# Scratch rows of four runs side by side, and an input read by four transfers for each half batch

## The chip, the cores and the metric

The kernel runs on one core of a Trainium2 chip. The metric is the device time of one execution in microseconds (us). Runs of the same kernel agree within some tenths of a per cent.

## What is computed

Two layers, one behind the other, in float32. The first is a causal convolution over time with a softmaxed kernel of 7 taps for each of 8 heads. The second is a layer of 8 experts in which the (token, expert) pairs are taken in the order of their gate values and an expert takes at most 3584 tokens.

```python
def _attn_ref(x, weight):             # x 8 x 3584 x 192, weight 8 heads x 7 taps
    w = softmax(weight)               # over the taps
    x_pad = np.concatenate([np.zeros((B, 6, D)), x], axis=1)
    ...
    out = np.einsum('hk,bskhg->bshg', w, x_unf)

def _moe_ref(x, w_gate, w1, w2):      # x 28672 x 192, 8 experts, inner width 1024
    order = np.argsort(-(x @ w_gate).flatten())
    for idx in order:                 # greedy, 3584 tokens to each expert
        ...
    for e in range(8):
        out[mask] = np.maximum(x[mask] @ w1[e], 0.0) @ w2[e]
```

## The kernel before, in words

**First stage.** The 28,672 tokens are worked on in 16 half batches of 1792 tokens, each as 16 windows of 112 tokens. `load(i)` (L182) brings half batch i into a tile X of 118 partitions x 16 windows x 192 numbers: partition p of window w holds token w * 112 + p - 6, so that the six tokens in front of a window stand in the first six partitions. There are three X tiles, and `load(i + 2)` stands ahead of `conv(i)` in the program. `conv(i, mid)` (L194) multiplies X, head by head, with a Toeplitz matrix TH of the taps (118 x 128) on TensorE; each of the 8 products has 384 columns and runs as two matmuls. ScalarE copies each product into the tile `a` (two of these), and its queue stores `a` as the scratch tensor `attn` in DRAM (L203). One row of `attn` is one token, 192 numbers or 768 bytes. VectorE transposes `a` for the gate's logits (`transp`, `logits`), which PE makes a half batch or two later; `mid(h)` puts these steps, and steps of the routing, between the matmuls of `conv`.

**Routing.** Generators (`half`, `rest`, `last`, L1357 to L1373) make the expert lists in small steps on VectorE, PE and ScalarE, in the background of the other work. A small planner (`Pace`, `Steps`) sums up what it holds each engine's time to be and so decides between which matmuls a step is put. At the end of each list, `tokens` (L533) turns sorted positions into token numbers `idx` (tiles ia0, ia, ib0 and ib), four times in the program.

**Experts.** Tiles of 512 tokens of one expert: GpSimd (POOL) gathers the tokens' rows from `attn` by `idx` with indirect DMAs (`gather`, L1170), PE and VectorE transpose them, two layers of matmuls follow (`ph` and `y` in the profile), and GpSimd scatters the result rows to the output by the same `idx` (`store`, L1236). Expert weights come in through SP's queue (`wload`, L1103), are split into two parts and kept in DRAM (`wsplit`, L1121) for a second pass over the experts.

**What sets the order.** Each engine works in program order. SP's queue holds the loads of X and all weight transfers, ACT's queue the stores to `attn`, POOL's queue the gathers and scatters. The first gather reads the first 14,336 rows of `attn`. Class `General` is a general path that runs only if the fast routing finds that it does not hold; for this input it doesn't run, but the change keeps it in step.

Nearly all instructions of PE, VectorE and ScalarE carry line 54 in the profile, where a helper records them, so they are told apart by their tiles: `cv` is the product of the convolution, `px` the transposed gathered rows, `xg` the gathered rows, `raw` loaded weights, `kw` and `kv` kept ones, `m_x`, `m_i`, `m_j` work tiles of `tokens`.

Of the kernel before, what the change touches and what calls it, by code (L numbers as in the profile page):

```python
# [5 lines left out]
F32 = mybir.dt.float32  # L6
# [10 lines left out]
G = 256  # L17
# [95 lines left out]
def build(ctx, tc, nc, x, weight, wg, attn, LT, wk):  # L113
# [68 lines left out]
    def load(i):  # L182
        t = X[i] = k.xp[i % 3].tile([118, 16, D], F32, name="X")
        b, hf = divmod(i, 2)
        o = x.offset + (b * 3584 + hf * 1792) * D
        if hf == 0:
            P.memset(t[0:6, 0], 0.0)
            nc.sync.dma_start(t[0:6, 1:16], bass.AP(tensor=x.tensor, offset=o + (W - 6) * D,
                                                    ap=[[D, 6], [W * D, 15], [1, D]]))
        else:  # L190
            nc.sync.dma_start(t[0:6], bass.AP(tensor=x.tensor, offset=o - 6 * D, ap=[[D, 6], [W * D, 16], [1, D]]))
        nc.sync.dma_start(t[6:118], bass.AP(tensor=x.tensor, offset=o, ap=[[D, W], [W * D, 16], [1, D]]))
# [12 lines left out]
    def transp(i, u):  # L205

# [54 lines left out]


class Route:

# [265 lines left out]
            V.tensor_tensor(self.asm[:, 0:16 * nt], self.asm[:, 0:16 * nt], ps, op=OP.add)  # L530
        yield

    def tokens(self, nt, idx, e1=8, t1=None):  # L533
# [10 lines left out]
        i = v(wk.tile([128, 128], I32, name="m_j"))  # L544
        off = wk.tile([128, 1], F32, name="off")
# [16 lines left out]
    def lists(self, F, nt, h, base, idx, *part):  # L562
# [6 lines left out]
        yield from self.tokens(nt, idx, *part)  # L569

    def counts(self, n0):

# [237 lines left out]
class General:  # L810


    def __init__(self, ctx, tc, ltab, attn, w1, w2, out, ident, drm):
        self.tc, self.nc, self.ltab = tc, tc.nc, ltab
        self.attn, self.w1, self.w2, self.out, self.ident = attn, w1, w2, out, ident
        self.p = ctx.enter_context(tc.tile_pool(name="gp", bufs=1))
        self.ps = ctx.enter_context(tc.tile_pool(name="gps", bufs=1, space=PSUM))
        self.list = drm.tile([NTOK, 1], I32, name="glist")

    def consts(self):  # L820
        nc, p = self.nc, self.p
# [19 lines left out]
        self.idi = p.tile([128, G], I32, name="g_idi")  # L841
        V.tensor_copy(self.idi, self.id)

        V.tensor_scalar(w, pi, 16, None, op0=OP.bitwise_and)
        wf = p.tile([128, 1], F32, name="g_wf")
# [128 lines left out]
    def lists(self):  # L974

        nc, tc, p = self.nc, self.tc, self.p
        V, PE = nc.vector, nc.tensor
        W = self.W
        rows = p.tile([128, 8], F32, name="g_rows")
        base = p.tile([128, 8], F32, name="g_base")  # L980
        sc = p.tile([128, G], F32, name="g_sc")
        one = p.tile([128, G], F32, name="g_one")
        slot = p.tile([128, G], F32, name="g_slot")
        V.memset(one, 1.0)
        V.memset(slot, 0.0)
# [12 lines left out]
        V.tensor_copy(si, slot)  # L998
        s1 = p.tile([128, 1], I32, name="g_s1")
        i1 = p.tile([128, 1], I32, name="g_i1")  # L1000
        with tc.For_i(0, G, 1) as g:
            V.tensor_copy(s1, si[:, bass.ds(g, 1)])
            V.tensor_copy(i1, self.idi[:, bass.ds(g, 1)])
            nc.gpsimd.indirect_dma_start(
                out=self.list, out_offset=bass.IndirectOffsetOnAxis(ap=s1, axis=0), in_=i1, in_offset=None,
                bounds_check=NTOK - 1, oob_is_err=False)

    def ffn(self):
# [5 lines left out]
        ix = p.tile([128, 1], I32, name="g_ix")  # L1014
# [7 lines left out]
        with tc.For_i(0, NE, 1) as e:  # L1022
# [3 lines left out]
            with tc.For_i(0, CAP // 128, 1) as t:  # L1026
                nc.sync.dma_start(ix, self.list[bass.ds(e * CAP + t * 128, 128)])
                P.indirect_dma_start(out=x, out_offset=None, in_=self.attn,
                                     in_offset=bass.IndirectOffsetOnAxis(ap=ix, axis=0),
                                     bounds_check=NTOK - 1, oob_is_err=False)  # L1030
                px = self.ps.tile([128, 512], F32, name="g_ps")
                PE.transpose(px[:, 0:128], x[:, 0:128], self.ident)
# [12 lines left out]
                P.indirect_dma_start(out=self.out, out_offset=bass.IndirectOffsetOnAxis(ap=ix, axis=0),  # L1045
                                     in_=y, in_offset=None, bounds_check=NTOK - 1, oob_is_err=False)

    def run(self):
# [5 lines left out]
class FFN:  # L1054
# [235 lines left out]
    def run(self, idx_of, at, eng, free):  # L1290
# [30 lines left out]
def moe_kernel(ctx, tc, x, weight, wg, w1, w2, out):  # L1321
# [6 lines left out]
    with ExitStack() as cw:  # L1328
# [14 lines left out]
        ib = lst.tile([128, 8, TB], I32, name="ib")  # L1343
        ib0 = lst.tile([128, NL, 4], I32, name="ib0")

        order = [(e, (0,)) for e in range(NE)]
        order += [(e, (1, 2)) for e in range(NE - 1, -1, -1)]
        order += [(e, (3,)) for e in range(NL)]
# [8 lines left out]
        def half(h):  # L1357
# [3 lines left out]
            yield from r.count(r.F, h)  # L1361
            if h:
                yield from r.counts(NE)
            yield from r.lists(r.F, TA, h, 0 if h else None, *((ia,) if h else (ia0, 8, 4)))

        def rest():
            yield from r.open()
            yield from r.rounds()
            yield from r.final(NL)
            yield from r.lists(r.F, TB, 1, None, ib0, NL, 4)  # L1370

        def last():
            yield from r.lists(r.F, TB, 0, 1, ib)  # L1373

        def tail():

# [114 lines left out]
        ff.hp = [pool(cw, "fh0", 1, **late), None]  # L1491
        ff.wpool(cw, 1)

        def idx_of(tile_):
            e, t = tile_[1]
            if t == 0:
                return [ia0[:, e, b:b + 1] for b in range(4)]
            if t < 3:
                if len(bg.gens) > 2:
                    bg.drain(2)  # L1500
                return [ia[:, e, 4 * t + b:4 * t + b + 1] for b in range(4)]
            if t == 3 and e < NL:
                if len(bg.gens) > 1:
                    bg.drain(1)
                return [ib0[:, e, b:b + 1] for b in range(4)]
            if bg.gens:
                bg.drain()
            return [ib[:, e, 4 * (t - 3) + b:4 * (t - 3) + b + 1] for b in range(4)]

        SS = (1.8, 3)  # L1510
        ff.bg = lambda: bg.hook(SS[0], 4, SS[1])
# [43 lines left out]
```

## Time and profile before

| | us |
|---|---|
| runs of before | 1328.0, 1328.93 and 1332.42; median 1328.93 |
| profiled execution, own time | 1324.88 |
| its span, first to last instruction | 1323.1 |
| PE busy | 1251.3 (95%) |
| DVE (VectorE) busy | 1005.2 (76%) |
| ACT (ScalarE) busy | 543.2 (41%) |
| POOL (GpSimd) busy | 540.1 (41%) |
| moved by DMA | 188.29 MB, 142 GB/s on the mean |

The profile is one execution. Busy shares are means over stages with different limits, so the windows and the waits of one stage say more than the table. Queue 1 is SP's, queue 10 ACT's, queue 0 GpSimd's; a queue's share is the time that its packets took, of 16 DMA engines. Where packets of two queues lie beside each other on an engine, the shares can add up to more than one.

### The profile page before, as it was taken

Reading aid. Unit: us, or ns where it says so; the run is one execution under the profiler, and the core shown is the slowest. Engines: PE = TensorE matmul, PEld = TensorE weight load, DVE = VectorE, ACT = ScalarE, POOL = GpSimd, SP = SyncE. Lnnn points to the kernel's source line nnn. Section 1 sums busy time; section 2 is a strip of 40 time slices with the busy share of each in tenths; the row PEclk is TensorE's granted clock in tenths of the full one; section 3 lists DMA queues with packets and bytes.
Section 4 is the critical chain, followed back from the end, with each engine's and each line's share of the span. In section 5 each row is a group of like instructions: output and inputs, shape, how many; then the busy total and the mean of one; then the engine's idle time right before and its main releaser. Section 6 shows DMA issues by size and latency. Waiting matters only on the chain.

```text
span 1323.1 us, 21760 instructions
## 1 busy us (share of the span) xinstructions
PE 1251.3 (95%) x7879; PEld 1077.4 (81%) x7879; DVE 1005.2 (76%) x2223; ACT 543.2 (41%) x1182; POOL 540.1 (41%) x547
## 2 busy tenths in 40 slices
PE   5888959999799999999999999999999999999997
PEld 2444637887789888888899999999999999999996
DVE  7369648779999988899757777777777777777772
ACT  4434434475444434443333333333333333333332
POOL 3000065586644434435224434444444444444422
PEclk9889989899899999999899999999999999999999
DMA  9999879488753433424222341432323222141100
GB/s 239 285 294 297 231 211 324 154 275 270 241 186 101 143 99 134 145 91 143 76 83 89 130 160 45 149 101 87 104 87 104 93 93 90 48 148 46 41 29 27
DMA packets 114434, 188.29 MB, mean 142 GB/s; under 512 B 12352, under 2 KB 86544, under 8 KB 110096
## 3 DMA queue, kind: packets, MB, share of 16 engines
q1 hardware_dynamic: 63888, 120.75, 28.4%
q0 software_dynamic: 21504, 44.07, 10.9%
q10 hardware_dynamic: 28928, 22.02, 5.2%
q8 instruction: 63, 1.03, 0.3%
q14 instruction: 51, 0.42, 0.1%
HBM read 114.44 MB, written 72.35 MB: 141 GB/s over the span
## 4 chain that ended last, share of the span: by engine, by line
PE 77%; DVE 9%; DMA 8%; issue 2%; POOL 2%; ACT 2%; SPq 1%; POOLq 0%; ACTq 0%; DVEq 0%
PE ph L54 34%; PE y L54 33%; DMA attn<-a 5%; PE cv L54 4%; PE bg L54 3%; DMA raw<-in_moe_w_dram 3%; DVE X L54 2%; DVE hl L54 2%; PE px L54 1%; PE pl L54 1%; DVE TH L54 1%; DVE oa L54 1%; POOL xg L1175 1%; POOL w L1156 1%; DVE r_w L54 0%
## 5 line engine op out<-in xcount | busy, mean ns | idle before, releaser
L54 PE MATMUL y<-w,hh 128*128 128x384 f32 x1792 | 543.6, 359 | 0.0
L54 ACT ACTIVATE hh<-ph 128x512 fp32r<-128x512 f32 x448 | 267.0, 596 | 492.3 <-PE ph L54 491.9
L54 PE MATMUL y<-w,hl 128*128 128x192 f32 x1792 | 451.3, 252 | 0.0
L54 DVE SCALAR_TENSOR_TENSOR hl<-ph,hh 128x512 fp32r<-128x512 f32 x448 | 308.2, 689 | 174.6 <-ACT hh L54 170.9
L54 PE MATMUL ph<-xa,w 128*128 128x512 f32 x1344 | 399.7, 406 | 2.3 <-DVE hl L54 2.3
L54 PEld LDWEIGHTS y<-w,hh 128*128 128x128 f32 x1792 | 339.4, 189 | 25.2 <-issue 7.5
L54 PEld LDWEIGHTS y<-w,hl 128*128 128x128 f32 x1792 | 344.0, 192 | 15.2
L1243 POOL DMA_INDIRECT out_dram<-yo,ib x128 | 128.0, 1000 | 294.2 <-DVE yo L54 279.4
L54 PEld LDWEIGHTS ph<-xa,w 128*128 128x128 f32 x1344 | 221.5, 191 | 22.7 <-DVE hl L54 2.9
L1243 POOL DMA_INDIRECT out_dram<-yo,ia x96 | 106.3, 1108 | 241.0 <-DVE yo L54 210.3
L54 DVE STREAM_TRANSPOSE xs<-xg 32x256 f32<-32x256 f32 (+1 forms) x512 | 188.8, 369 | 8.8
L54 PE MATMUL ph<-xd,w 128*128 128x512 f32 x448 | 179.7, 401 | 0.0
L54 PE MATMUL ph<-xd,dl 128*128 128x512 f32 x448 | 175.8, 392 | 1.2 <-DVE dl L54 1.2
L1175 POOL DMA_INDIRECT xg<-attn,ib x128 | 129.7, 1013 | 40.1 <-issue 39.8
L54 PE MATMUL cv<-X,TH 118*128 118x384 f32 x256 | 103.8, 539 | 31.1 <-ACT a L54 18.4
L1175 POOL DMA_INDIRECT xg<-attn,ia x96 | 106.8, 1112 | 28.9 <-issue 23.2
L54 ACT ACTIVATE yt<-y 128x192 f32<-128x192 f32 x224 | 73.3, 327 | 108.2 <-PE y L54 105.2
L54 DVE TENSOR_TENSOR yo<-y,yt 128x192 f32<-128x192 f32 x224 | 79.7, 356 | 42.1 <-ACT yt L54 39.3
L54 PEld LDWEIGHTS ph<-xd,dl 128*128 128x128 f32 x448 | 85.1, 190 | 21.6 <-DVE dl L54 2.6
L54 PEld LDWEIGHTS cv<-X,TH 118*128 118x128 f32 x256 | 48.0, 206 | 66.0 <-ACT a L54 26.7
L54 PEld LDWEIGHTS ph<-xd,w 128*128 128x128 f32 x448 | 85.2, 190 | 20.1 <-DVE xd L54 0.7
L54 ACT ACTIVATE a<-cv 128x384 f32<-128x384 f32 x128 | 59.2, 491 | 66.2 <-DMA attn<-a 36.8
(230 smaller groups left out, 966.6 us busy)
## 6 DMA issues: line engine op xcount, KB each, us to landing
w<-kw SPq DMA_DIRECT2D x16, 1536.0 KB
w<-kv SPq DMA_DIRECT2D x16, 1536.0 KB
X<-in_x_dram SPq DMA_DIRECT2D x16, 1344.0 KB
attn<-a ACTq DMA_DIRECT2D x16, 1344.0 KB
kw<-w SPq DMA_DIRECT2D x48, 256.0 KB
kv<-w SPq DMA_DIRECT2D x32, 384.0 KB
raw<-in_moe_w_dram SPq DMA_DIRECT2D x32, 192.0 KB
raw<-in_moe_w_dram SPq DMA_DIRECT2D x16, 256.0 KB
```

Of the source, the lines that this page charges most:

```text
L54: return f(*a, **k)
L1156: eng.tensor_tensor(lo, r[0:n], hi[0:n].bitcast(F32), op=OP.subtract)
L1175: self.nc.gpsimd.indirect_dma_start(out=t[:, b], out_offset=None, in_=self.attn[0:rows], in_offset=bass.IndirectOffsetOnAxis(ap=idx[b], ax ...
L1243: st = nc.gpsimd.indirect_dma_start(out=self.out, out_offset=bass.IndirectOffsetOnAxis(ap=idx, axis=0), in_=o, in_offset=None, bounds_chec ...
```

## The change

1. `attn` keeps the same bytes, but its rows are laid out anew: window w = 4g + b, partition p, half batch i stands at row 1792 i + 448 g + 4 p + b, so four windows' tokens of one partition stand side by side. The store of a half batch then writes 112 x 4 pieces of 768 numbers (3072 bytes) in place of 112 x 16 pieces of 768 bytes.
2. Gathers need the row in `attn`, scatters the token. `tokens` makes both: `idx` as before, and `row` (tiles ja0, ja, jb0, jb) by four more VectorE operations. `idx_of(tile, True)` hands out rows.
3. `load(i)` reads all 118 partitions by four transfers of four windows each. In the first half batch of each of the 8 sequences, the first window, which has no tokens in front, is read alone over 112 partitions, and the first of the four transfers has three windows. The separate transfers over 6 partitions are gone.

```diff
@@ def load(i)
         o = x.offset + (b * 3584 + hf * 1792) * D
+        x_ = lambda w, n, p: bass.AP(tensor=x.tensor, offset=o + (w * W + p - 6) * D, ap=[[D, 118 - p], [W * D, n], [1, D]])
+
+        parts = [(4 * c, 4) for c in range(4)]
         if hf == 0:
             P.memset(t[0:6, 0], 0.0)
-            nc.sync.dma_start(t[0:6, 1:16], bass.AP(tensor=x.tensor, offset=o + (W - 6) * D,
-                                                    ap=[[D, 6], [W * D, 15], [1, D]]))
-        else:
-            nc.sync.dma_start(t[0:6], bass.AP(tensor=x.tensor, offset=o - 6 * D, ap=[[D, 6], [W * D, 16], [1, D]]))
-        nc.sync.dma_start(t[6:118], bass.AP(tensor=x.tensor, offset=o, ap=[[D, W], [W * D, 16], [1, D]]))
+            nc.sync.dma_start(t[6:118, 0:1], x_(0, 1, 6))
+            parts[0] = (1, 3)
+        for w, n in parts:
+            nc.sync.dma_start(t[:, w:w + n], x_(w, n, 0))
@@ def conv(i, mid)
-        A.dma_start(attn[i * 1792:(i + 1) * 1792].rearrange("(w p) d -> p w d", p=W), a[0:W])
+        A.dma_start(attn[i * 1792:(i + 1) * 1792].rearrange("(g p b) d -> p g (b d)", g=4, b=4),
+                    a[0:W].rearrange("p (g b) d -> p g (b d)", b=4))
@@ def tokens(self, nt, idx, row, ...)
+        V.scalar_tensor_tensor(y, i, -127.0 / 4, x, op0=OP.mult, op1=OP.add)
         V.scalar_tensor_tensor(x, i, 80.0, x, op0=OP.mult, op1=OP.add)

         V.tensor_scalar(gi, f, -1.0, off, op0=OP.add, op1=OP.add)
+        V.scalar_tensor_tensor(y, gi, 28.0, y, op0=OP.mult, op1=OP.add)
         V.tensor_scalar(i, gi, 3, None, op0=OP.bitwise_and)
         V.scalar_tensor_tensor(x, gi, 112.0, x, op0=OP.mult, op1=OP.add)
         V.scalar_tensor_tensor(idx, i, -80.0, x, op0=OP.mult, op1=OP.add)
+        V.scalar_tensor_tensor(y, i, 4.0, y, op0=OP.mult, op1=OP.add)
+        V.tensor_scalar(row, y, 4.0, None, op0=OP.mult)
@@ def run(self, idx_of, at, eng, free)
-                self.gather(i + 2, idx_of(tiles[i + 2]))
+                self.gather(i + 2, idx_of(tiles[i + 2], True))
@@ def first(e)
-            ff.gather(e, [ia0[:, e, b:b + 1] for b in range(4)], NTOK // 2, V)
+            ff.gather(e, [ja0[:, e, b:b + 1] for b in range(4)], NTOK // 2, V)
```

The first rows of SP's queue before: the loads of the first six half batches, with the small gate weights between (shapes are partitions x windows x numbers).

```order
1 L123 DMA wb<-in_weight_dram 128x56
2 L188 DMA X<-in_x_dram 6x15x192
3 L192 DMA X<-in_x_dram 112x16x192
4 L191 DMA X<-in_x_dram 6x16x192
5 L192 DMA X<-in_x_dram 112x16x192
6 L166 DMA wgr<-in_moe_w_gate_dram 32x6x8 x4
7 L188 DMA X<-in_x_dram 6x15x192
8 L192 DMA X<-in_x_dram 112x16x192
9 L191 DMA X<-in_x_dram 6x16x192
10 L192 DMA X<-in_x_dram 112x16x192
```

The same place now:

```order
1 L123 DMA wb<-in_weight_dram 128x56
2 L191 DMA X<-in_x_dram 112x192
3 L194 DMA X<-in_x_dram 118x3x192
4 L194 DMA X<-in_x_dram 118x4x192 x7
5 L166 DMA wgr<-in_moe_w_gate_dram 32x6x8 x4
6 L191 DMA X<-in_x_dram 112x192
7 L194 DMA X<-in_x_dram 118x3x192
8 L194 DMA X<-in_x_dram 118x4x192 x7
```

Two half batches were four transfers and are nine: no transfer has 6 partitions any more, and all but one of the nine have 118. What stands behind the loads on this queue is the same.

VectorE at the end of the first list before, on the way to the first gather (`asm` is the sorted list, `ia` the token numbers):

```order
144 L54 TENSOR_TENSOR m_f<-asm,m_f 128x32
145 L54 SCALAR_TENSOR_TENSOR m_x<-m_j,m_x 128x32
146 L54 TENSOR_SCALAR m_i<-m_f,off 128x32
147 L54 TENSOR_SCALAR m_j<-m_i 128x32
148 L54 SCALAR_TENSOR_TENSOR m_x<-m_i,m_x 128x32
149 L54 SCALAR_TENSOR_TENSOR ia_105<-m_j,m_x 128x32
150 L54 STREAM_TRANSPOSE aT<-a 128x768
```

The same place now (`ja` is the list of rows):

```order
144 L54 TENSOR_TENSOR m_f<-asm,m_f 128x32
145 L54 SCALAR_TENSOR_TENSOR m_y<-m_j,m_x 128x32
146 L54 SCALAR_TENSOR_TENSOR m_x<-m_j,m_x 128x32
147 L54 TENSOR_SCALAR m_i<-m_f,off 128x32
148 L54 SCALAR_TENSOR_TENSOR m_y<-m_i,m_y 128x32
149 L54 TENSOR_SCALAR m_j<-m_i 128x32
150 L54 SCALAR_TENSOR_TENSOR m_x<-m_i,m_x 128x32
151 L54 SCALAR_TENSOR_TENSOR ia_105<-m_j,m_x 128x32
152 L54 SCALAR_TENSOR_TENSOR m_y<-m_j,m_y 128x32
153 L54 TENSOR_SCALAR ja_109<-m_y 128x32
154 L54 STREAM_TRANSPOSE aT<-a 128x768
```

The list is four operations longer, and the gather reads `ja`, the last of them. On PE the same instructions stand in the same order, but for a few background steps that are put some matmuls later at two places behind the first stage.

More of the change, by code (lines that the diff above doesn't have):

```diff
@@ L531, in gather, with tokens @@
         yield
-    def tokens(self, nt, idx, e1=8, t1=None):
+    def tokens(self, nt, idx, row, e1=8, t1=None):
         nc, wk = self.nc, self.wk
@@ L544, in tokens @@
         i = v(wk.tile([128, 128], I32, name="m_j"))
+        y = v(wk.tile([128, 128], F32, name="m_y"))
         off = wk.tile([128, 1], F32, name="off")
@@ L559, in tokens, with lists @@
         V.scalar_tensor_tensor(idx, i, -80.0, x, op0=OP.mult, op1=OP.add)
+        V.scalar_tensor_tensor(y, i, 4.0, y, op0=OP.mult, op1=OP.add)
+        V.tensor_scalar(row, y, 4.0, None, op0=OP.mult)
         yield
-    def lists(self, F, nt, h, base, idx, *part):
+    def lists(self, F, nt, h, base, idx, row, *part):
         nc = self.nc
@@ L568, in lists @@
         yield from self.gather(nt, base is None)
-        yield from self.tokens(nt, idx, *part)
+        yield from self.tokens(nt, idx, row, *part)
     def counts(self, n0):
@@ L817, in __init__ @@
         self.ps = ctx.enter_context(tc.tile_pool(name="gps", bufs=1, space=PSUM))
-        self.list = drm.tile([NTOK, 1], I32, name="glist")
+        self.list = drm.tile([NTOK, 2], I32, name="glist")
     def consts(self):
@@ L840, in consts @@
         V.tensor_scalar(self.id, self.id, pt, None, op0=OP.add)
-        self.idi = p.tile([128, G], I32, name="g_idi")
-        V.tensor_copy(self.idi, self.id)
+        self.idi = p.tile([128, G, 2], I32, name="g_idi")
+        V.tensor_copy(self.idi[:, :, 0], self.id)
+        V.tensor_scalar(f3, gi, 28.0, None, op0=OP.mult)
+        V.scalar_tensor_tensor(f3, g3, 4.0, f3, op0=OP.mult, op1=OP.add)
+        V.tensor_scalar(pt, w, -127.0 / 4, None, op0=OP.mult)
+        V.tensor_tensor(pt, pt, pi, op=OP.add)
+        V.tensor_scalar(self.idi[:, :, 1], f3, pt, 4.0, op0=OP.add, op1=OP.mult)
         V.tensor_scalar(w, pi, 16, None, op0=OP.bitwise_and)
@@ L999, in lists @@
         s1 = p.tile([128, 1], I32, name="g_s1")
-        i1 = p.tile([128, 1], I32, name="g_i1")
+        i1 = p.tile([128, 2], I32, name="g_i1")
         with tc.For_i(0, G, 1) as g:
             V.tensor_copy(s1, si[:, bass.ds(g, 1)])
-            V.tensor_copy(i1, self.idi[:, bass.ds(g, 1)])
+            V.tensor_copy(i1, self.idi[:, bass.ds(g, 1)].rearrange("p o c -> p (o c)"))
             nc.gpsimd.indirect_dma_start(
@@ L1013, in ffn @@
         b = p.tile([128, 8, D], F32, name="g_wb")
-        ix = p.tile([128, 1], I32, name="g_ix")
+        ix = p.tile([128, 2], I32, name="g_ix")
         x = p.tile([128, D], F32, name="g_x")
@@ L1028, in ffn @@
                 P.indirect_dma_start(out=x, out_offset=None, in_=self.attn,
[L1029 removed]
+                                     in_offset=bass.IndirectOffsetOnAxis(ap=ix[:, 1:2], axis=0),
                                      bounds_check=NTOK - 1, oob_is_err=False)
@@ L1044, in ffn @@
                 V.tensor_copy(y, py[:, 0:D])
-                P.indirect_dma_start(out=self.out, out_offset=bass.IndirectOffsetOnAxis(ap=ix, axis=0),
+                P.indirect_dma_start(out=self.out, out_offset=bass.IndirectOffsetOnAxis(ap=ix[:, 0:1], axis=0),
                                      in_=y, in_offset=None, bounds_check=NTOK - 1, oob_is_err=False)
@@ L1344, in moe_kernel @@
         ib0 = lst.tile([128, NL, 4], I32, name="ib0")
+        ja0 = lst.tile([128, 8, 4], I32, name="ja0")
+        ja = lst.tile([128, 8, TA], I32, name="ja")
+        jb = lst.tile([128, 8, TB], I32, name="jb")
+        jb0 = lst.tile([128, NL, 4], I32, name="jb0")
         order = [(e, (0,)) for e in range(NE)]
@@ L1363, in half @@
                 yield from r.counts(NE)
-            yield from r.lists(r.F, TA, h, 0 if h else None, *((ia,) if h else (ia0, 8, 4)))
+            yield from r.lists(r.F, TA, h, 0 if h else None, *((ia, ja) if h else (ia0, ja0, 8, 4)))
         def rest():
@@ L1369, in rest @@
             yield from r.final(NL)
-            yield from r.lists(r.F, TB, 1, None, ib0, NL, 4)
+            yield from r.lists(r.F, TB, 1, None, ib0, jb0, NL, 4)
         def last():
-            yield from r.lists(r.F, TB, 0, 1, ib)
+            yield from r.lists(r.F, TB, 0, 1, ib, jb)
         def tail():
@@ L1492, in moe_kernel, with idx_of @@
         ff.wpool(cw, 1)
-        def idx_of(tile_):
+        def idx_of(tile_, rows=False):
             e, t = tile_[1]
             if t == 0:
-                return [ia0[:, e, b:b + 1] for b in range(4)]
+                return [(ja0 if rows else ia0)[:, e, b:b + 1] for b in range(4)]
             if t < 3:
@@ L1500, in idx_of @@
                     bg.drain(2)
-                return [ia[:, e, 4 * t + b:4 * t + b + 1] for b in range(4)]
+                return [(ja if rows else ia)[:, e, 4 * t + b:4 * t + b + 1] for b in range(4)]
             if t == 3 and e < NL:
@@ L1504, in idx_of @@
                     bg.drain(1)
-                return [ib0[:, e, b:b + 1] for b in range(4)]
+                return [(jb0 if rows else ib0)[:, e, b:b + 1] for b in range(4)]
             if bg.gens:
                 bg.drain()
-            return [ib[:, e, 4 * (t - 3) + b:4 * (t - 3) + b + 1] for b in range(4)]
+            return [(jb if rows else ib)[:, e, 4 * (t - 3) + b:4 * (t - 3) + b + 1] for b in range(4)]
         SS = (1.8, 3)
```

## The prediction

> **What bounds the kernel now.** I read the busy shares by slice first, then what TensorE (PE) and ScalarE (ACT) wait for in the first stage, then the DMA queues of that stage. The windows of one slice each (columns: length, busy time and instructions of PE, PEld, DVE, ACT, POOL, then the granted clock, the DMA engines' share and GB/s):
>
> ```profile
> 0.00:33.10 33.10, 17.19 (x64) 8.93 (x64) 23.28 (x75) 14.26 (x32) 10.05 (x41) 1.00 0.98 239
> ...
> 99.20:132.30 33.10, 28.16 (x249) 15.46 (x248) 31.03 (x69) 13.54 (x33) 1.45 (x3) 0.95 1.02 297
> ...
> 397.00:430.00 33.00, 33.00 (x199) 29.78 (x198) 30.23 (x72) 15.84 (x40) 15.50 (x15) 1.00 0.31 101
> ```
>
> From the start to about 132 us the 16 DMA engines are full (share 0.98 to 1.02) and PE has gaps. From about 400 us PE is full and the DMA is not. The change touches the transfers of the first stage, so it is in that stage that it has to be priced. Who waits (total, times, longest): PE up to 160.6 us, ACT up to 172 us, and SP's queue and PE over the whole span:
>
> ```profile
> PE cv L54 <- ACT a L54: 18.4, 6, 6.2
> ...
> PE cv L54 <- DMA X<-in_x_dram: 0.4, 1, 0.4
> ```
>
> ```profile
> ACT a L54 <- DMA attn<-a: 36.8, 8, 9.3
> ```
>
> ```profile
> SPq L192 <- DMA attn<-a: 19.5, 4, 7.5
> ```
>
> ```profile
> PE px L54 <- DMA xg<-attn,ia: 10.0, 1, 10.0
> ```
>
> The convolution (cv) hardly ever waits for its input X (0.4 us in all). It waits for ACT, which waits 36.8 us for a buffer `a` whose store to the scratch has not landed. So today the loads keep ahead, and the stores are what is late. The last half batch's 16 cv matmuls stand in these rows of PE's timeline (start, length, tile, count: 4 + 2 + 6 + 4 = 16):
>
> ```profile
> 160.65 1.46 PE L54 MATMUL cv<-X,TH 118*128 118x384 f32 x4
> ...
> 162.95 0.86 PE L54 MATMUL cv<-X,TH 118*128 118x384 f32 x2
> ...
> 165.04 2.18 PE L54 MATMUL cv<-X,TH 118*128 118x384 f32 x6
> ...
> 167.94 1.56 PE L54 MATMUL cv<-X,TH 118*128 118x384 f32 x4
> ```
>
> Behind 160.65 us lie 1323.1 - 160.65 = 1162.5 us of span, which no load of X reaches into.
>
> **How many engines a transfer gets.** This is the term on which everything else hangs, so I count packets. I read the small ones as the end of a transfer, one on each engine that carried a part of it. The DMA queues of the first 7 us, and two rows of the whole span:
>
> ```profile
> DMA packets 1398, 0.99 MB, mean 141 GB/s; under 512 B 150, under 2 KB 1398, under 8 KB 1398
> ```
>
> ```profile
> q1 hardware_dynamic: 63888, 120.75, 28.4%
> ...
> q10 hardware_dynamic: 28928, 22.02, 5.2%
> ```
>
> In those 7 us the small packets are 150. The weights' transfer brings 128 rows of 56 numbers (224 B), which leaves 22 = 16 + 6: sixteen that close the transfer over 128 partitions, and six that close the one of L188, over 6 partitions. Queue 10 holds only the 16 stores: 16 x 112 x 16 rows make 28,672, and the other 256 are 16 for each store. So 128 partitions were on 16 engines with 8 each, 112 on 16 with 7 each, and 6 on 6 with one each, although L188 has 90 rows that could have fed all 16. All three are cuts into equal shares of whole partitions. The new loads stand over 118 partitions, and 118 = 2 x 59: up to 16 engines, only 2 (or 1) get equal shares. I take **two engines**. The Trainium skill (DMA: Bandwidth & Descriptors, section Why a DMA increments its semaphore by 16 and not by 1) states that such a transfer is spread over the largest number up to 16 that divides the slowest dimension of both its sides, with 100 partitions on 10 engines and 127 on 1 as examples; by that rule 118 come on 2. The trace agrees for 6, 112 and 128; no row here shows 118.
>
> **Part by part.**
>
> *Loads.* Removed are 16 loads over 6 partitions and 16 over 112. Added are 64 over 118 partitions and 8 single windows over 112. The rows stay the same in number: 248 windows x 118 rows + 8 x 112 = 30,160, as 28,672 + 1,488 before. On two engines the 248 x 118 = 29,264 rows of 768 B are 22.47 MB, 11.24 MB each; the single windows add 8 x 112 x 768 B / 16 = 0.04 MB.
>
> *Stores.* Still 112 partitions, so 16 engines, but in pieces of 3072 B: 7,168 packets for 28,672. By the time the last load is in, 14 of 16 stores have gone through, 22.02 x 14/16/16 = 1.20 MB on each engine. So each of the two engines carries 11.24 + 0.04 + 1.20 = 12.48 MB before cv of the last half batch can start.
>
> The rate of an engine, from DMA queues in four windows (10 to 20, 26 to 37, 0 to 138 and 365 to 369 us; packets, MB, share of 16 engines):
>
> ```profile
> DMA packets 3686, 2.20 MB, mean 220 GB/s; under 512 B 855, under 2 KB 3686, under 8 KB 3686
> ...
> q1 hardware_dynamic: 3686, 2.20, 112.3%
> ```
>
> ```profile
> DMA packets 5352, 4.08 MB, mean 371 GB/s; under 512 B 41, under 2 KB 5352, under 8 KB 5352
> ```
>
> ```profile
> DMA packets 51138, 38.31 MB, mean 278 GB/s; under 512 B 1491, under 2 KB 51128, under 8 KB 51128
> ...
> q1 hardware_dynamic: 29432, 21.66, 62.2%
> q10 hardware_dynamic: 21696, 16.52, 36.5%
> ```
>
> ```profile
> q1 hardware_dynamic: 372, 1.04, 66.2%
> ```
>
> Loads alone, on all 16 engines, moved 220 GB/s, 13.8 an engine. Loads and stores together moved 371, 23.2 an engine, with the same 768 B pieces. The mean to 138 us is 278, 17.4 an engine. Pieces of 3072 B (the kept weights' writes) moved 1.04 MB in 0.662 x 16 x 4 = 42.4 engine-us, 24.5 an engine. I take 23.2: it shows what an engine does with 768 B pieces when nothing else holds it up, and the slow 220 came when 16 engines read at once, while two engines ask for 46 GB/s in all. So 12.48 MB / 23.2 GB/s = 538 us, from about 2.5 us on, when the first rows move. cv of the last half batch then starts at **540.5 us** in place of 160.65. Between, each half batch takes 538/16 = 34 us, and cv with its stores (8.9 us from 160.65 to 169.5 now) hides in that; nothing else in the stage is as late. Three X buffers keep one to two loads queued ahead, so I cost gaps between loads at nothing. If that cover went, the 19.5 us that SP waits for store landings now are what a gap of that kind costs.
>
> *Waits.* SP's queue holds the weights' first loads behind the last X load, before and after; their parts on the two busy engines land just behind X. Nothing waits for them before cv of the last half batch.
>
> *Row lists.* Each of the four lists gets four more DVE operations (three on `m_y`, one into the row list), one of which a gather then waits for. Their like:
>
> ```profile
> 166.32 0.19 DVE L54 SCALAR_TENSOR_TENSOR m_x<-m_j,m_x 128x32 f32<-128x32 int32 x1
> ...
> 167.02 0.19 DVE L54 SCALAR_TENSOR_TENSOR ia<-m_j,m_x 128x32 int32<-128x32 int32 x1
> ```
>
> 4 x 0.19 = 0.8 us stand ahead of the first gather, for which PE already waits 10.0 us: 0.8 us on the path. The other three lists lie under PE's full stretches. The gathers read the same rows of 768 B from other places; I cost that at nothing, since rows of one gather are scattered either way. Behind 400 us PE hides it (share of the DMA 0.31). A few background steps stand a little later on PE and DVE behind the stage: nothing, to a microsecond or two either way.
>
> *Behind the stage.* The 1162.5 us stay, with less in the way: the transfers that PE and ACT wait for there (10.0 us for the first gather, and two weight loads in the chain) meet emptier queues:
>
> ```profile
> 186.65 3.07 DMA raw<-in_moe_w_dram
> 196.93 6.26 DMA raw<-in_moe_w_dram
> ```
>
> At best 10.0 + 3.07 + 6.26 = 19 us come back; I take none, since the gather itself and the weights' own time stay.
>
> **Sum.** 540.5 + 1162.5 + 0.8 = 1703.8 us of span, and 1324.88 - 1323.1 = 1.8 around it: 1705.6. The profiled execution (1324.88) is 4 us, 0.3%, under the median of the runs (1328.93); with those 4 us, **1710 us**. About 0.3% is also what a measurement of this kernel can tell from no change.
>
> **The rivals.**
>
> *Two engines, but each as slow as when loads run alone.* If the 13.8 GB/s belong to the engine (the time that one read takes) and not to the crowd of 16, the stage takes 12.48/13.8 = 904 us and the run 904 + 2.5 + 1162.5 + 0.8 + 1.8 + 4 = 2076 us. For it: the two engines will carry loads nine parts in ten, as in 10 to 20 us. Against it: at 371 GB/s the same loads took their half of an engine without slowing it. Rates in between give times in between: 17.4 GB/s gives 717 + 2.5 + 1169 = 1889.
>
> *All 16 engines, in unequal shares (seven or eight partitions each): faster.* Then the loads cost what they cost now, and the stores gain: 36.5% x 16 x 138 = 806 engine-us for 16.52 MB are 20.5 GB/s an engine, against 24.5 for 3072 B pieces. 22.02 MB over 16 engines take 67 us at the one and 56 at the other, 11 us less, and store landings are what ACT waits for: 1318 us. It decides from about ten engines up: below, 22.47 MB over so few engines and 1.2 MB of stores at 23.2 GB/s don't fit into the 158 us that they have now. For it: nothing shown, beside that no 118 was ever seen. Against it: 6 partitions on 6 engines. The Trainium skill (same page, section Specifications) has 512 B as the least piece for full rate, so that by it 768 B stores would gain nothing and this case would give 1329 us; the 20.5 and 24.5 of the trace speak against that.
>
> *All 16, and the gain hidden.* Around 150 us PE has work without a pause, so earlier stores there bring nothing: 1329 us, no change.
>
> **Chances.** Two engines near full rate (17.4 to 24.5 GB/s): 0.80. Two engines, slower: 0.11. Sixteen, faster: 0.06. Sixteen, no change: 0.03. The range goes from the fast end, 12.48/24.5 = 509 us, with the 19 us given back (509 + 2.5 + 1162.5 + 0.8 + 5.8 - 19 = 1661), to 17.4 GB/s (1889); the other three cases, 0.20, are left out. Slower 0.91, the same 0.03, faster 0.06.
>
> **What would show it.** Queue 1 tells the engine count: the X loads close with 16 x 16 + 16 x 6 = 352 small packets now; with two engines it is 64 x 2 + 8 x 16 = 256, so 63,792 packets in place of 63,888; with sixteen 64,688. Queue 10 should hold 7,168 + 256 = 7,424. The DMA share should lie near 0.2 up to about 540 us, at some 78 GB/s (22.47 MB loaded and 19.3 MB stored in 538 us), with cv waiting for X some 25 us in each half batch. A full DMA share in the first slices, or 64,688 packets, would make the forecast wrong; 63,792 packets with a stage of 700 us or more would leave the step right and the rate wrong.

## The result and the profile after

| | before | after |
|---|---|---|
| median of 6 runs, us | 1330.74 (1328.0 to 1332.42) | 1730.97 (1728.49 to 1734.61) |
| profiled execution, us | 1324.88 | 1732.32 |
| its span, us | 1323.1 | 1730.2 |

The ratio is 1.3011, 95% interval [1.2987, 1.3036]. The forecast was 1710 us, 1661 to 1889: right in direction and mechanism, 21 us too low.

The two queues that were to tell the engine count hold (packets, MB, share of 16 engines):

```profile
q1 hardware_dynamic: 63792, 120.75, 20.7%
...
q10 hardware_dynamic: 7424, 22.02, 3.7%
```

Both counts are those forecast for two engines, to the packet. The windows of the changed kernel, the first three at the times of before's and one in the experts' stage (columns as in the prediction):

```profile
0.00:33.10 33.10, 0.00 (x0) 0.00 (x0) 15.13 (x56) 6.52 (x16) 6.21 (x20) 1.00 0.14 43
99.20:132.30 33.10, 9.63 (x65) 5.03 (x65) 4.12 (x6) 4.09 (x9) 0.00 (x0) 0.65 0.14 46
397.00:430.00 33.00, 10.31 (x83) 5.71 (x83) 7.85 (x15) 4.25 (x10) 1.20 (x2) 0.66 0.26 85
800.00:833.00 33.00, 32.89 (x196) 29.52 (x195) 29.66 (x70) 15.27 (x40) 15.55 (x15) 1.00 0.32 101
```

The DMA share, 0.98 to 1.02 before, is 0.14 here, and PE, which ran 28.16 of 33.1 us at 99.20, runs 9.63. The window in the experts' stage looks like before's at 397 us, only later. The DMA queues from the start to 555 us, and what PE waits for in the whole span:

```profile
DMA packets 38669, 44.20 MB, mean 80 GB/s; under 512 B 1552, under 2 KB 31712, under 8 KB 38655
...
q1 hardware_dynamic: 32000, 24.27, 13.7%
q10 hardware_dynamic: 6655, 19.76, 10.4%
```

```profile
PE cv L54 <- DMA X<-in_x_dram: 350.7, 14, 35.2
...
PE cv L54 <- ACT a L54: 18.5, 1, 18.5
...
PE bg L54 <- ACT oa L54: 9.7, 1, 9.7
```

80 GB/s were forecast as 78, and the wait for X is 350.7/14 = 25 us for each of 14 half batches, as forecast. The wait for `oa`, a tile of the routing's sort, is to be kept in mind: 9.7 us here, and before:

```profile
PE bg L54 <- ACT oa L54: 4.7, 2, 3.9
```

The chain of waits, its shares by engine, and three of its pieces in order of time (start, length, what):

```profile
PE 56%; SPq 32%; DVE 6%; issue 2%; DMA 2%; ACT 1%; POOL 1%; POOLq 0%; DVEq 0%; ACTq 0%
```

```profile
518.71 8.11 SPq L194
...
526.86 7.77 SPq L194
...
534.67 10.86 SPq L1125
```

SP's queue, 1% of the chain before, is 32% now. The first two rows are the last two loads of X, the third is a weight transfer, and each is held for about 8 or 11 us. I read this as the time until there is room for its packets behind the earlier ones; the profile doesn't say it. A transfer of four windows has 4 x 118 = 472 rows, 236 for each of two engines: in 8.11 us that is 34.4 ns for 768 B, or 22.3 GB/s an engine, the rate at which the loads drain.

The end of the stage on PE, and the first gather on POOL:

```profile
540.29 2.93 PE L54 MATMUL cv<-X,TH 118*128 118x384 f32 x4 [18.55 <-ACT a L54]
...
546.08 2.90 PE L54 MATMUL cv<-X,TH 118*128 118x384 f32 x4
...
552.66 2.90 PE L54 MATMUL cv<-X,TH 118*128 118x384 f32 x4 [1.97 <-DMA raw<-in_moe_w_dram]
```

```profile
564.52 1.25 POOL L1189 DMA_INDIRECT xg<-attn,ja  x1 [0.59 <-DVE xg L54]
```

The same gather before, for the sums below:

```profile
170.39 1.25 POOL L1175 DMA_INDIRECT xg<-attn,ia  x1 [0.17 <-issue]
```

The profile puts the last conv's wait of 1.97 us down to a weight load, but this conv reads only X and TH. In the trace the last transfer of X lands at 552.46 us, and that fits as well. This conv begins at 552.66 us and the first gather at 564.52, so the spans fall into three parts:

| us | before | forecast | after | off by |
|---|---|---|---|---|
| start to the last conv | 160.65 | 540.5 | 552.66 | +12.2 |
| last conv to the first gather | 9.74 | 10.5 | 11.86 | +1.3 |
| first gather to the end | 1152.71 | 1152.7 | 1165.68 | +13.0 |
| span | 1323.1 | 1703.8 | 1730.2 | +26.4 |

So two terms are off, the length of the stage and what lies behind the first gather, each by 0.7% or 0.8% of the run. The experiments ask whether the equal shares are the cause of the 400 us, and then where these two come from.

### The profile page after: what moved, and what is told of

Its sections match the earlier page's. It is cut to its first block, busy times and chain, and to the rows that moved or that the text cites. A ratio compares the mean times of both kernels' runs of the same rounds, so it can differ in the third digit from the quotient of the medians.

```text
span 1730.2 us, 21834 instructions
## 1 busy us (share of the span) xinstructions
PE 1280.7 (74%) x7879; PEld 1091.8 (63%) x7879; DVE 1005.1 (58%) x2239; ACT 541.5 (31%) x1182; POOL 542.9 (31%) x547
## 3 DMA queue, kind: packets, MB, share of 16 engines
q1 hardware_dynamic: 63792, 120.75, 20.7%
q10 hardware_dynamic: 7424, 22.02, 3.7%
## 4 chain that ended last, share of the span: by engine, by line
PE 56%; SPq 32%; DVE 6%; issue 2%; DMA 2%; ACT 1%; POOL 1%; POOLq 0%; DVEq 0%; ACTq 0%
SPq L194 27%; PE ph L54 26%; PE y L54 26%; SPq L191 3%; PE bg L54 2%; DVE X L54 2%; DVE hl L54 1%; DMA raw<-in_moe_w_dram 1%; PE px L54 1%; SPq L1125 1%; POOL w L1170 1%; SPq L166 1%; ACT a_d L54 1%; DVE oa L54 0%; DMA xg<-attn,ja 0%
## 5 line engine op out<-in xcount | busy, mean ns | idle before, releaser
L54 PE MATMUL cv<-X,TH 118*128 118x384 f32 x256 | 129.2, 652 | 397.6 <-DMA X<-in_x_dram 350.7
L54 PEld LDWEIGHTS cv<-X,TH 118*128 118x128 f32 x256 | 59.2, 250 | 442.4 <-issue 409.9
L1189 POOL DMA_INDIRECT xg<-attn,jb x128 | 129.7, 1013 | 40.1 <-issue 39.8
L1189 POOL DMA_INDIRECT xg<-attn,ja x96 | 108.4, 1129 | 29.3 <-issue 24.1
L54 DVE TENSOR_TENSOR LT<-pt,pm 128x128 f32<-128x128 f32 x14 | 4.0, 286 | 182.6 <-PE pt L54 182.6
```

Of the source, the lines that this page charges most:

```text
L54: return f(*a, **k)
L1189: self.nc.gpsimd.indirect_dma_start(out=t[:, b], out_offset=None, in_=self.attn[0:rows], in_offset=bass.IndirectOffsetOnAxis(ap=idx[b], ax ...
```

## The experiments

Each kernel ran beside the kernel before on the same chip, which gave 1322 to 1328 us there; the ratios are the figures to compare.

| kernel | median, us | ratio to before, 95% interval |
|---|---|---|
| old loads, rest as changed | 1328.54 | 0.9993 [0.9967, 1.0019] |
| loads over 120 partitions | 1326.71 | 0.9986 [0.9958, 1.0013] |
| over 128 | 1318.75 | 0.9921 [0.989, 0.9953] |
| over 119 | 1382.74 | 1.0389 [1.0331, 1.0447] |
| over 124 | 1496.78 | 1.1268 [1.1221, 1.1315] |
| over 118, one transfer a half batch | 1736.4 | 1.3084 [1.3032, 1.3137] |
| first weights from ACT's queue | 1735.16 | 1.3066 [1.3022, 1.311] |
| matmuls ahead of the last conv | 1733.96 | 1.306 [1.3016, 1.3104] |
| changed, order of before | 1722.6 | 1.3004 [1.2957, 1.3051] |
| old loads, order of before | 1313.71 | 0.9936 [0.9907, 0.9964] |
| 128 partitions, order of before | 1304.43 | 0.9867 [0.9828, 0.9906] |
| stores from POOL's queue | 1731.54 | 1.308 [1.3053, 1.3107] |

### The loads undone

`load` as before, the new scratch rows and stores kept:

```diff
-        for w, n in parts:
-            nc.sync.dma_start(t[:, w:w + n], x_(w, n, 0))
+            nc.sync.dma_start(t[0:6], bass.AP(..., ap=[[D, 6], [W * D, 16], [1, D]]))
+        nc.sync.dma_start(t[6:118], bass.AP(..., ap=[[D, W], [W * D, 16], [1, D]]))
```

> The changed kernel with the loads of before (6 and 112 partitions), so only the new scratch rows and the second row list are left of the change. Theory A (a load gets only as many engines as cut its partitions into equal shares, so 118 get two): the whole loss is gone, and the stores' larger pieces remain, 1315 to 1331 us, at best 11 us under before. Theory B (the loss comes from the number of transfers, each of which holds SP's queue for some 8 us): also 1315 to 1331. If the new scratch rows or the longer lists cost something by themselves, it shows here: over 1335.

The 400 us are gone: all of them come from the loads. The stores did get cheaper. A row of the DMA queues to 138 us, one of ACT's waits to 150 us and the first gather:

```profile
q10 hardware_dynamic: 5695, 16.91, 32.9%
```

```profile
ACT a L54 <- DMA attn<-a: 13.7, 3, 6.4
```

```profile
164.51 1.25 POOL L1187 DMA_INDIRECT xg<-attn,ja  x1 [0.58 <-DVE xg L54]
```

0.329 x 16 x 138 = 726 engine-us for 16.91 MB are 23.3 GB/s an engine, where the 768 B pieces had 20.5, and ACT waits 13.7 us for store landings in place of 34.5 in that stretch. The first gather, at 164.51 us, is 5.9 us earlier than before. Yet the run is no faster. The same loss as in the changed kernel lies behind the first gather: 1327.9 - 164.51 = 1163.4 us to the end, 10.7 more than before's 1152.7. This is taken up again further below.

### Other partition counts

X is read over 120, 128, 119 or 124 partitions: each window brings 2, 10, 1 or 6 more tokens in front of its six, whose rows of TH are zero, so that the result stays the same. For 128:

```diff
-        V.tensor_scalar(MK[:, j], D0[:, 0:W], float(j), None, op0=OP.is_equal)
+        V.tensor_scalar(MK[:, j], D0[:, 0:W], float(j + 10), None, op0=OP.is_equal)
-        t = X[i] = k.xp[i % 3].tile([118, 16, D], F32, name="X")
+        t = X[i] = k.xp[i % 3].tile([128, 16, D], F32, name="X")
-   ... offset=o + (w * W + p - 6) * D, ap=[[D, 118 - p], ...
+   ... offset=o + (w * W + p - 16) * D, ap=[[D, 128 - p], ...
-            P.memset(t[0:6, 0], 0.0)
+            P.memset(t[0:16, 0], 0.0)
-            PE.matmul(ps[:, 0:384], TH[0:118, h], ...
+            PE.matmul(ps[:, 0:384], TH[0:128, h], ...
```

> The changed kernel with two more tokens in front, so that every load has 120 partitions instead of 118, with as many transfers and 1.7% more bytes (the Toeplitz matrix is shifted by two rows, the result is the same). Theory A: 120 = 15 x 8, fifteen engines; each carries 1.52 + 1.24 = 2.76 MB, 119 us at 23.2 GB/s, less than the 158 us that the stage has, so the time is that of the old loads, 1315 to 1331 us. Theory B: the same number of transfers, 1731 us or a little more.

> As the run with 120 partitions, but with ten more tokens in front, 128 partitions. Theory A: 128 = 16 x 8, sixteen engines, 8.5% more bytes than 118: 1315 to 1331 us, within some microseconds of 120 partitions, and SP's issues take well under 1 us each. Theory B: 1731 us or more.

> As the run with 120 partitions, but with one more token in front only, 119 partitions. Theory A: 119 = 17 x 7, seven engines; each carries 3.24 + 1.24 = 4.48 MB, 193 us at 23.2 GB/s, so that the last convolution starts at about 196 instead of 161 us: 1366 to 1393 us, with up to 27 us behind the stage as with two engines. Queue 1 then closes each of the 64 loads with seven small packets: 64 x 7 + 8 x 16 = 576. Theory B: 1731 us. A split into unequal shares over all engines would make 1315 to 1331.

> As the run with 120 partitions, but with six more tokens in front, 124 partitions. Theory A: 124 = 31 x 4, four engines; each carries 5.90 + 1.24 = 7.15 MB, 308 us at 23.2 GB/s, the last convolution starts at about 310 us: 1481 to 1508 us. Theory B (number of transfers): 1731 us. So more partitions than 119 or 120, but a slower kernel by Theory A alone.

Queue 1 of the kernels with 120, 128, 119 and 124 partitions, in this order:

```profile
q1 hardware_dynamic: 65120, 121.13, 28.3%
```

```profile
q1 hardware_dynamic: 67168, 122.66, 27.6%
```

```profile
q1 hardware_dynamic: 64360, 120.94, 25.8%
```

```profile
q1 hardware_dynamic: 65408, 121.89, 23.9%
```

In the changed kernel 63,792 - 30,160 rows of X - 256 leaves 33,376 packets for everything else on this queue. Take off those and the rows of X (248 windows x partitions + 896), and what is left are the packets that close the loads. 119 partitions: 64,360 - 33,376 - 30,408 = 576 = 128 + 64 x 7. 124: 384 = 128 + 64 x 4. 120: 1088 = 128 + 64 x 15. 128: 1152 = 128 + 64 x 16. So 119 = 7 x 17 is on seven engines, 124 = 4 x 31 on four, 120 on fifteen, 128 on sixteen: equal shares of whole partitions, the largest number of engines up to 16. One partition more takes two engines to seven, and some 350 us off the run. The Trainium skill's rule (DMA: Bandwidth & Descriptors, section Why a DMA increments its semaphore by 16 and not by 1) gives these same counts, and the traces agree in all five.

The last conv of the kernels with 119 and with 124 partitions starts at

```profile
206.55 2.77 PE L54 MATMUL cv<-X,TH 119*128 119x384 f32 x4
```

```profile
318.43 1.46 PE L54 MATMUL cv<-X,TH 124*128 124x384 f32 x4
```

Neither row waited for X. PE was still at half batch 14, which ACT had held up by 3.9 us (119) and 6.4 us (124) with a late store, of which more below. In the traces the last row of X is moved by 198.6 and 313.1 us, 8.0 and 5.4 us earlier. An engine has carried 4.41 MB by then with seven engines and 7.11 MB with four, the stores so far included: 4.41/196.1 = 22.5 and 7.11/310.6 = 22.9 GB/s. With two engines, where the last row is moved by 551.9 us, it is 12.48/549.4 = 22.7. From two to seven engines the rate of one hardly depends on their number.

The kernel with 128 partitions moves 1.92 MB more than the kernel before and is 0.8% faster than it. Four things differ there from the old loads (sixteen engines for all rows, no separate transfers over 6 partitions, four transfers in place of one, matmuls over 128 rows); they were not taken apart.

### One transfer of 118 partitions

```diff
-        parts = [(4 * c, 4) for c in range(4)]
+        parts = [(0, 16)]
...
-            parts[0] = (1, 3)
+            parts[0] = (1, 15)
```

> The changed kernel with one transfer over 118 partitions for each half batch (16 windows, or 15 beside the single one) instead of four. Theory A: still two engines and the same bytes, so 1731 us to within 15. Theory B (each transfer costs some 8 us of SP's queue): a quarter of the transfers, so three quarters of the 400 us come back, about 1430 us.

The number of transfers is not the cause: 1736.4 us with 24 of them in place of 72. One row of SP's queue:

```profile
99.88 35.20 SPq L191 DMA_DIRECT2D X<-in_x_dram  x1
```

L191 is the load of a single window, 112 rows over 16 engines, and it is held for 35 us. In front of it stands a half batch of 16 windows, four times what stood in front of an instruction that was held for 8.1 us. So SP's hold follows the rows ahead in the queue, not the instruction that is held. It is a symptom of the slow drain and not its cause.

### The 12 us at the end of the stage

Three edits to the changed kernel try to bring back parts of the 26 us. The first takes the weights' first transfers off SP's queue. The second is to keep PE busy ahead of the last conv, since PE's granted clock is 0.50 there:

```diff
+        dq = nc.scalar if self.loaded < 4 else nc.sync
-            nc.sync.dma_start(t, self.w1[e, 0:128, s])
+            dq.dma_start(t, self.w1[e, 0:128, s])
```

> The changed kernel with the first four weight pieces (six transfers) issued from ACT's queue instead of SP's, where they stand behind the blocked loads until 535 us. Theory of the 27 us lost behind the stage, first half (the first weights come late, since SP's queue is blocked): they land before the last convolution, some 10 to 14 us come back, 1717 to 1721 us. Rival (the 27 us come from PE's lower granted clock after its idle time, or from the queue order further on): 1728 to 1734, no change.

```diff
+            if i == 15:
+                for _ in range(10):
+                    z = k.cps.tile([128, 512], F32, name="cv")
+                    nc.nc.tensor.matmul(z[:, 0:384], k.TH[:, 0], ...
```

> The changed kernel with ten matmuls of the Toeplitz matrix with itself (128 x 384, their result is not used) put on PE ahead of the last half batch's convolution, where PE now sits idle for 18.5 us. Second half of that theory (PE's granted clock is 0.50 in the 10 us after the idle time and makes the last convolution slow): the convolution and the steps between its matmuls take about 9 to 14 us instead of 23, 1717 to 1724 us. Rival (PE waits there for what other engines bring): 1728 to 1736 us.

Neither gains anything. PE in the first and in the second of them:

```profile
547.50 2.92 PE L54 MATMUL cv<-X,TH 118*128 118x384 f32 x4 [20.60 <-ACT a L54]
```

```profile
550.65 7.77 PE L1486 MATMUL cv<-TH 128*128 128x384 f32 x20
558.26 1.46 PE L54 MATMUL cv<-X,TH 118*128 118x384 f32 x4
```

In the first, ACT stands in the weight transfers too, and half batch 14 goes on 7 us later (547.50 for 540.29). So this run can't tell whether the late weights cost something. In the second, the added matmuls did not lie in a pause: the long pause is in the middle of half batch 14, behind a store that ACT issues late. They ran on the path and put the last conv 5.6 us later. The clock idea was right in kind: the first four matmuls took 1.46 us in place of 2.90, at a granted clock of 1.00 in place of 0.50, and from the last conv to the first gather it took 10.14 us in place of 11.86. But that is worth 1.7 us, not the 7 to 14 that were expected.

That pause itself, 18.55 us, was the next suspect. One line puts the stores on POOL's queue:

```diff
-        A.dma_start(attn[i * 1792:(i + 1) * 1792].rearrange(...
+        P.dma_start(attn[i * 1792:(i + 1) * 1792].rearrange(...
```

> The changed kernel with one line changed: the stores to the scratch are issued from GpSimd's queue, which has no other work in this stage, and not from ScalarE's. Theory S (the held store): in the changed kernel ScalarE stood in the store of a half batch until 539.32 us, so conv of half batch 14 stopped in its middle (18.5 us) and the last conv began at 552.66 us. With the store on another queue half batch 14 is done by about 530 us, the last conv begins when its X is in, at some 545 us, and about 7 us come back: 1724 us. Theory N: the end of the stage is set by the last X rows and the weights behind them, not by the store: 1731, and the last conv begins within 2 us of 552.7. If the other queue is held in the same way, PE's wait for a stays at some 18 us and nothing changes.

PE's timeline of this kernel, and SP's:

```profile
524.74 2.18 PE L54 MATMUL cv<-X,TH 118*128 118x384 f32 x6
529.15 1.54 PE L54 MATMUL cv<-X,TH 118*128 118x384 f32 x4
556.13 2.90 PE L54 MATMUL cv<-X,TH 118*128 118x384 f32 x4 [23.83 <-DMA X<-in_x_dram]
```

```profile
538.67 10.83 SPq L1125 DMA_DIRECT2D raw<-in_moe_w_dram  x1
```

The pause is gone: half batch 14 is done at 530.7 us, as the theory of the held store had it. But no time is gained, and the theory that the pause costs time falls: the last conv now waits 23.83 us for its own X and begins 17.5 us after SP got rid of the last load (556.13 - 538.67). In the changed kernel that distance is 18.0 us (552.66 - 534.67). So the held store only filled time in which the last rows were still on their way, and what ends the stage is the drain of two engines. The 12.2 us are then the rate: 22.7 GB/s where the sum had 23.2. Why SP's last load itself stands 4 us later in this kernel is open.

What held the store can be read from the trace. The transfers of SP and ACT take turns on eight semaphores, counters by which a transfer reports that it has landed, and one that is to use a semaphore waits until the earlier transfer on it has landed. In the changed kernel ACT was free at 496.93 us, but its store shares a semaphore with the third load of half batch 15, issued by SP at 518.71 us. That load lands at 539.24, and the store goes out at 539.32. The first 15 of the 16 stores there start so, each within 0.1 us of the landing of such a load. Stores from POOL's queue use other semaphores, and the pause goes with them. With 119 and 124 partitions the same wait lay on the path, since X was in before half batch 14 was done.

### The 13 us behind the first gather

The kernel with the old loads showed 10.7 us of it without any of the slow stage. The trace of the changed kernel has a place for it, ACT's timeline after the first gathers (`w` is the first half of a split weight):

```profile
592.13 0.63 ACT L54 ACTIVATE w<-raw 128x512 fp32r<-128x512 f32 x1 [8.42 <-issue]
...
593.84 0.63 ACT L54 ACTIVATE w<-raw 128x512 fp32r<-128x512 f32 x1
...
595.66 0.63 ACT L54 ACTIVATE w<-raw 128x512 fp32r<-128x512 f32 x1 [0.71 <-DMA raw<-in_moe_w_dram]
...
596.92 0.63 ACT L54 ACTIVATE w<-raw 128x512 fp32r<-128x512 f32 x1
597.46 0.26 ACT L54 ACTIVATE oa<-bg 128x128 f32<-128x128 f32 x1
```

`oa` stands behind four `w`. The first of them starts after 8.42 us of idle time and the others as their weights arrive, so `oa` comes at 597.46, and PE waits 9.7 us for it. In the kernel before, the same `oa` stands behind one:

```profile
196.95 0.63 ACT L54 ACTIVATE w<-raw 128x512 fp32r<-128x512 f32 x1 [6.20 <-issue]
197.49 0.26 ACT L54 ACTIVATE oa<-bg 128x128 f32<-128x128 f32 x1
```

The planner made the difference: it counts the four new VectorE operations, holds VectorE to be late, and lets the next steps of the routing wait for some more matmuls. Three kernels issue these four operations past the planner's count, and nothing else:

```diff
+        U = nc.nc.vector
-        V.scalar_tensor_tensor(y, i, -127.0 / 4, x, op0=OP.mult, op1=OP.add)
+        U.scalar_tensor_tensor(y, i, -127.0 / 4, x, op0=OP.mult, op1=OP.add)
...
-        V.tensor_scalar(row, y, 4.0, None, op0=OP.mult)
+        U.tensor_scalar(row, y, 4.0, None, op0=OP.mult)
```

PE's and ACT's instructions then stand word for word in the order of before, and VectorE's differ by the added operations alone.

> The changed kernel, with its four added VectorE operations of `tokens` still run, but not counted by the planner, so that the order of PE's instructions is word for word that of the kernel before. Theory P: the planner, told of four more operations, moved steps of the routing on PE and ScalarE, and that move costs the 9 to 13 us that appear between the first gather and some 300 us behind it (in the kernel with the old loads 3 + 5.9 = 8.9 us). Then 1731 - 9 = 1722 us, and PE waits 4 to 5 us for oa, not 9.7. Theory G: the gathers read scattered rows of the new layout more slowly, whatever the order: 1731, and the shift behind the first gather stays.

> The old loads with the new rows and stores, the four operations not counted by the planner. Theory P: 1328.5 - 9 = 1320 us, 0.6% faster than the kernel before: the 5.9 us that the stores gain in the first stage stay. Theory G: 1328.5, no difference from the kernel before.

> Loads over 128 partitions, the four operations not counted by the planner. Theory P: 1318.75 - 9 = 1310 us, ratio 0.986, the best of all kernels here. Theory G: 1318.75 again.

ACT in the first of the three, and PE's wait for `oa`:

```profile
589.89 0.63 ACT L54 ACTIVATE w<-raw 128x512 fp32r<-128x512 f32 x1 [6.07 <-issue]
590.43 0.26 ACT L54 ACTIVATE oa<-bg 128x128 f32<-128x128 f32 x1
```

```profile
PE bg L54 <- ACT oa L54: 3.9, 1, 3.9
```

`oa` is behind one `w` again and PE waits 3.9 us, 5.8 less. PE's wait for `hl`, a tile that VectorE makes between an expert's two layers, shrinks too. It is 6.5 us in the changed kernel, in the first row, and 2.1 in this one:

```profile
PE ph L54 <- DVE hl L54: 6.5, 3, 3.9
```

```profile
PE ph L54 <- DVE hl L54: 2.1, 2, 1.8
```

The first gather of the three, in the same order:

```profile
564.88 1.25 POOL L1190 DMA_INDIRECT xg<-attn,ja  x1 [0.58 <-DVE xg L54]
```

```profile
158.07 1.25 POOL L1188 DMA_INDIRECT xg<-attn,ja  x1 [0.58 <-DVE xg L54]
```

```profile
153.99 1.25 POOL L1190 DMA_INDIRECT xg<-attn,ja  x1 [0.58 <-DVE xg L54]
```

From there to the end (spans 1720.9, 1309.8 and 1302.0) it is 1156.0, 1151.7 and 1148.0 us, against 1165.7 in the changed kernel and 1152.7 before. In the ten kernels that keep the planner's count this stretch is 1159.4 to 1167.4 us. So 9.7 of the 13.0 us are the planner's order, and the two waits, 5.8 + 4.4 us, are about as much. The theory of slower gathers falls: with the old loads and the old order the gathers read the new rows, and this stretch is 1.0 us shorter than before. The ratios say the same where they are fine enough: with the old loads 0.9993 goes to 0.9936, with intervals apart, and with 128 partitions 0.9921 to 0.9867, with intervals that just overlap. For 118 partitions 1.3011 and 1.3004 have intervals of half a per cent and can't tell; there only the trace does. The remaining 3.3 us (1156.0 - 1152.7) stay open.

The kernel with 128 partitions and the old order is the fastest of all: 1304.43 us beside 1322.26, 1.3% less than before.

## Why the prediction was right, and where its sum was off

*How many engines a transfer gets.* Right. 63,792 packets on queue 1 and 7,424 on queue 10 were forecast to the packet, and four more partition counts follow the same equal shares.

*Each of the two engines carries 12.48 MB.* Nothing speaks against it: the rates worked out in this way for two, four and seven engines, 22.7, 22.9 and 22.5 GB/s, agree within 2%.

*The rate, 23.2 GB/s.* The step that was mis-sized. It measured 22.7, which makes the stage 12.2 us longer. The 371 GB/s it was taken from are the best stretch of a mix with stores. What speaks for two engines reading alone is this window of the changed kernel:

```profile
530.00:540.00 10.00, 0.00 (x0) 0.00 (x0) 0.00 (x0) 0.25 (x1) 0.00 (x0) 0.50 0.14 45
```

45 GB/s are 22.5 an engine. This also settles the first rival: 13.8 GB/s is not what an engine does with loads alone. Nor is it what sixteen always do: 855 of the 3686 packets behind that figure were small ones, and with 128 partitions sixteen engines moved 355 GB/s of loads alone from 8 to 10 us, 22.2 each.

*Gaps between loads at nothing.* Right. SP's queue is held nearly all the time up to the last load, so the two engines have the next load behind the present one.

*Waits: nothing waits for the weights behind the last X.* Not contradicted: the weights issued from another queue brought nothing. But that kernel also held ACT longer, so it doesn't show that they are free.

*Row lists: 0.8 us ahead of the first gather.* The stretch from the last conv to the first gather grew by 2.1 us. The lists are 0.4 of it: with the old loads, whose last conv starts at 154.36 us, it is 10.15 us in place of 9.74. The rest, 1.7 us, is a term that the sum did not have: the last conv takes 10.55 us in place of 8.85 from its first matmul to its last, and its first four matmuls run at a granted clock of 0.50, behind PE's idle time.

*"A few background steps stand a little later on PE and DVE behind the stage: nothing, to a microsecond or two either way."* This step failed. The moved steps cost 9.7 us. On ACT, where the sum did not look, one of them came to stand behind three more weight conversions, which made 5.8 us of it.

*The second rival, 16 engines and stores 11 us cheaper.* Its mechanism for 118 partitions fell. Its sum for the stores is borne out in the main where sixteen engines do read most of the rows: 20.5 to 23.3 GB/s (24.5 in the sum), and with the order put back 0.64% [0.36, 0.93] less time, some 8 us (11 in the sum).

*From the profiled execution to the median.* 4 us were added since before's profile lay under its median. After's profile lies 1.4 us above its median, so this term turned round, and the point is 21 us low where the span is 26.4 us low. The misses of the stage and of what lies behind it went the same way, so but for these 5 us the forecast doesn't owe its nearness to errors that cancel.

## What to carry to other kernels

Look at the divisors of the partition count before a transfer is made one: 118 = 2 x 59 cost 30%, while a pad to 128 moved more bytes and was 0.8% faster than the kernel before. Where a planner sets the order, an operation that costs 0.2 us can move others by many microseconds, so compare the order on every engine and look what the moved step comes to stand behind. When a stage is bound by a drain, a pause that ends before the drain does is worth nothing, however long it looks in the waits.

## What the runs showed of the hardware that was not expected

- A DMA instruction on SP's queue can last as long as the engines take to drain what stands ahead of it: 8.1 us behind 236 rows of 768 B on each of two engines, 35 us behind four times as many, for most loads of X 0.3 us before. Its length shows the drain rate.
- An engine moved 22.5 to 22.9 GB/s, nearly all of it in 768 B reads, whether two, four or seven of them carried X.
- PE's granted clock was 0.50 behind the waits at the end of the stage, and four matmuls of the convolution took 2.90 us there, 1.46 at 1.00.
